# Turned tokens one tile a place, conversions shared from the fifth chunk on, and an overflow list in ten steps

## The chip, the cores and the metric

The kernel runs on one core of a Trainium2 chip. The metric is device time in microseconds (us) of one execution, the median of several. The core's engines run side by side, each through its own queue in order: TensorE (PE, matrix products, with weight loads PEld), VectorE (DVE), ScalarE (ACT), GpSimd (POOL) and SyncE (SP, which issues DMA transfers). An instruction that waits holds everything behind it on its engine.

## The reference

Clustered attention feeds a layer of 16 experts (4 groups of 4). A query attends only to keys of its own cluster; then every token goes to one expert, a two-layer network with ReLU, weighted by two softmax values:

```
mask = q_assign[:, :, :, None] == k_assign[:, :, None, :]
attn = softmax(where(mask, scale * q @ k.T, -1e9)) ; x = attn @ v     # 3072 tokens of 512
g_idx = argmax(x @ w_group) ; e_idx = argmax(xg @ w_expert[g])
h = np.maximum(xg[mask_e] @ w1[g, e], 0.0)                            # 512 -> 1024
out[tok_idx] = (g_w * e_w)[:, None] * (h @ w2[g, e])                  # 1024 -> 512
```

## The kernel before

Attention runs first, up to about 400 us. The expert stage is what the change touches. Float32 values are carried as two float16 parts, a high and a low one, so each product is three matmuls (high by high, high by low, low by high).

The first expert's 288 tokens of the first three batches are computed by `part_a`. Then `ranks` (L1421) goes over the remaining work in "ranks": rank -1 is a tile of 128 tokens of that first expert, ranks 0 to 14 are the other experts by falling size (288, 272, 256, 240, 232, 224, 216, 208, 200, 192 ... tokens). The body of a rank has eight places, i = 0 to 7. At each place PE computes one eighth of the rank's hidden layer (`up`, L1193, into one of three PSUM banks psh, evicted by ACT as hh, L1195, and by DVE as hl, L1196) and one eighth of the rank before's second layer (`down`, L1215 into one of two banks psy, evicted as yh on ACT and yl on DVE, L1219; some ranks take the form of L1229). At place 2 (place 6 of rank -1) `settle` turns the finished output back (L1251, into one of three banks psm), ACT scales it (y, L1257), and POOL scatters it to memory.

Weights come through `stream` (L994). Every expert has 16 chunks of 512 KB, loaded by SP (L951) into 13 lent places some way ahead; a chunk's place is free again when the chunk is split. Splitting (`split_chunk`, L972) takes two instructions: a conversion to the high part, on ACT (L978) or on POOL (L980), and the low part on DVE (L981). Chunks are counted from 0 here. `HI` alternates the two engines, but only from chunk `LEAD` = 12 on; chunks 0 to 11 are converted on ACT alone. Chunks 0 to 3, 4, 5, 8 and 9 are first-layer weights (wh0a, then wh0b), chunks 6, 7, 10 and 11 second-layer weights (wh1b). One chunk is split at each place.

A rank's tokens are gathered by POOL (L1150) from memory, token by token, and have to be turned for the products: PE transposes a tile of up to 128 tokens into a psm bank (L1165, or L1163 for a short one), and ACT copies it to xT (L1166; on DVE for the second tile in rank -1). `tokens` (L1168) does all tiles of the next rank at place `TOK` = 5, two or three of them.

For tokens that found no slot, DVE makes a list of further work (`lists` and `make_list`), in steps that ranks 2 and up take one at a time at place 3. Its long instructions work on 697 values of a single partition. The list is in eight steps: make_list's are taken in ranks 4 to 7, a test of the attention's sums in ranks 8 and 9.

The order in which instructions stand in an engine's queue is not the order of the code: a scheduler places them by its own estimate of times, under the `issue_after` constraints.

Of the kernel before, what the change touches and what calls it, by code (L numbers as in the profile page):

```python
# [11 lines left out]
F16 = mybir.dt.float16  # L12
# [10 lines left out]
P = 128  # L23
# [864 lines left out]
class Experts:  # L888
# [6 lines left out]
    short = ()  # L895
    AHEAD, MORE, AT = 9, 4, 8
    SLT = 13
    FILL, SETTLE, TOK = (0, 1, 2, 3, 4, 5, 6, 7), 2, 5
    HI = (0, 1, 0, 1, 0, 1, 0, 1)
    LEAD = 12  # L900

    def __init__(self, ctx, tc, R, w1, w2, out, stage, wa):
        self.tc, self.R, self.w1, self.w2, self.out = tc, R, w1, w2, out
# [212 lines left out]
    def stream(self):  # L1116
# [5 lines left out]
        for n in range(len(parts)):  # L1122
# [7 lines left out]
            if st is None:  # L1130
                yield
                continue
            self.split_chunk(st, *self.weights_of(r, i), i, q, self.HI[n % 8] if n >= self.LEAD else 0)
            self.ready = 4 * r + q + 1 if i == 0 else self.ready
# [32 lines left out]

    def tokens(self, xgs, M, beside=False):  # L1168
        nc = self.nc
        xT = self.xp.tile([P, 2, self.R.KD, M], F16, name="xT")  # L1170
        for t, xg in enumerate(xgs):
            self.transposed(xT, xg, t, min(P, M - t * P), self.R.psm.tile([P, 512], F32, name="psm"), nc.vector.tensor_copy if beside and t % 2 == 1 or M == P else nc.scalar.copy)
        return xT

    def ffn(self, xT, M, W, gcols, idcols):
        h = []
# [193 lines left out]
    def make_list(self):  # L1370
        nc, R = self.nc, self.R
        EB, MJ, MO = R.E + 1, R.N // P + 1, self.MO
        V = nc.vector
        V.tensor_tensor(out=self.Lrem, in0=self.c17[0:1], in1=self.done, op=ALU.subtract)
        V.tensor_tensor(out=self.Lgj, in0=self.Lrem.broadcast_to([1, EB, MJ]), in1=self.jt, op=ALU.is_gt)
        V.tensor_reduce(out=self.Lnov, in_=self.Lgj, axis=AX.X, op=ALU.add)
        V.tensor_tensor_scan(out=self.LhiE, data0=self.Lnov, data1=self.Lzer, initial=0.0, op0=ALU.add, op1=ALU.add)
        V.tensor_tensor(out=self.LloE, in0=self.LhiE, in1=self.Lnov, op=ALU.subtract)
        yield
        b3 = lambda x: x.unsqueeze(1).broadcast_to([1, MO, EB])  # L1380
        V.tensor_tensor(out=self.Lind, in0=self.jj, in1=b3(self.LloE), op=ALU.is_ge)
        V.tensor_tensor(out=self.Ltmp, in0=self.jj, in1=b3(self.LhiE), op=ALU.is_lt)
        V.tensor_tensor(out=self.Lind, in0=self.Lind, in1=self.Ltmp, op=ALU.mult)
        yield
        V.tensor_tensor(out=self.Ltmp, in0=self.Lind, in1=b3(self.eid), op=ALU.mult)
        V.tensor_reduce(out=self.Llst[:, 0], in_=self.Ltmp, axis=AX.X, op=ALU.add)
        yield

        V.tensor_tensor(out=self.Lsb, in0=self.base, in1=self.done, op=ALU.add)
        V.scalar_tensor_tensor(out=self.Lsb, in0=self.LloE, scalar=-float(P), in1=self.Lsb, op0=ALU.mult, op1=ALU.add)  # L1390
        V.scalar_tensor_tensor(out=self.Ltmp, in0=self.jj, scalar=float(P), in1=b3(self.Lsb), op0=ALU.mult, op1=ALU.add)
        V.scalar_tensor_tensor(out=self.Ltmp, in0=self.Ltmp, scalar=1.0 / 8, in1=self.Lind, op0=ALU.mult, op1=ALU.mult)
        V.tensor_reduce(out=self.Llst[:, 1], in_=self.Ltmp, axis=AX.X, op=ALU.add)
        V.tensor_copy(out=self.Llsi, in_=self.Llst)
        V.tensor_copy(out=self.Lnoi, in_=self.LhiE[:, EB - 1:EB])
        yield
# [24 lines left out]
    def ranks(self, bg):  # L1421

        E, sizes = self.R.E, self.sizes
        xT, xgs, down = self.xTB, self.xg0, iter(())
        for k in range(-1, E - 1):
            M = self.caps[k] if k >= 0 else P
            if 0 <= k < E - 2:
                xgs = self.gathers(k + 1)
            h = []
            up = self.up(xT, M, self.weights_of(k, 0) if k >= 0 else self.WA[0:2], h)  # L1430
            for i in range(8):
                while k >= 0 and self.ready < 4 * k + (4 if i >= 4 else 2) or k > 0 and self.ready2 < 4 * k - 4 + (4 if i >= 4 or not self.feature_major(self.caps[k - 1]) else 2):
                    next(self.fill)
                next(up, None)
                next(down, None)
                if i == (self.SETTLE if k >= 0 else 6):
                    if k == E - 2:
                        self.tc.keep_in_program_order(self.nc.gpsimd.drain())
                    self.settle()
                if i in self.FILL:  # L1440
                    with ExitStack() as order:
                        for op in (self.got, self.yev[min(1 + i // 2, 3)]) if k < 0 else (self.ev,):
                            order.enter_context(self.tc.issue_after(op.ins))
                        next(self.fill, None)
                if i == self.TOK and k + 1 < E - 1:
                    with self.tc.issue_after(self.mm.ins):
                        nT = self.tokens(xgs, self.caps[k + 1], k < 0)
                if k > 1 and i == 3:
                    with self.tc.issue_after(self.ev.ins):
                        next(bg, None)  # L1450
            for s in (up, down):
                for _ in s:
                    pass
            xT = nT
            if k >= 0:
                cols = [(self.gates[0:m, t, k:k + 1], self.ids[0:m, t, k:k + 1]) for t, m in enumerate(sizes[k])]
                down = self.down(h, M, self.weights_of(k, 1), [g for g, _ in cols], [i for _, i in cols])
            else:
                down = self.down(h, M, self.W2, [self.gB], [self.idB])
        for _ in self.fill:  # L1460
            pass
        for i, _ in enumerate(down):
            if i == 0:
                self.settle()
        self.settle()
        for _ in bg:
            pass

    def rest(self):
        self.again = True  # L1470
        nc, R, E, xp = self.nc, self.R, self.R.E, self.xp
        n_ov = nc.values_load(self.Lnoi[0:1, 0:1], min_val=0, max_val=self.MO)
        tabv = R.table.rearrange("(r s) w -> r s w", s=8)
        with self.tc.For_i(0, n_ov, 1) as j:
            er = self.load_reg(self.Llsi[0:1, 0, bass.ds(j, 1)], E - 1)
            tr = self.load_reg(self.Llsi[0:1, 1, bass.ds(j, 1)], (E + 1) * R.BS // 8 - P // 8)
            W = self.weights(er)
            tg = xp.tile([P, 2], F32, name="tg", bufs=1)
            nc.sync.dma_start(out=tg, in_=tabv[bass.ds(tr, P // 8)].rearrange("r s w -> (r s) w"))
            tid = xp.tile([P, 1], I32, name="tid", bufs=1)  # L1480
            nc.vector.tensor_copy(out=tid, in_=tg[:, 0:1])
            gt = xp.tile([P, 1], F32, name="gt", bufs=1)
            nc.vector.tensor_scalar(out=gt, in0=tg[:, 1:2], scalar1=1.0 / (XS * WS * WS), scalar2=None, op0=ALU.mult)
            xT = self.tokens([self.gather(tid, P)], P)
            for _ in self.ffn(xT, P, W, [gt], [tid]):
                pass

# [82 lines left out]
def tile_cluster_attention_moe(ctx, tc, qT, kT, vr, cen, wr, w1, w2, out):  # L1570
# [3 lines left out]
    E = w1.shape[0]  # L1574
# [17 lines left out]
    X = Experts(ctx, tc, R, w1, w2, out, stage, wa)  # L1592
# [15 lines left out]
    for i, _ in enumerate(ga):  # L1608
        with tc.issue_after(X.mm.ins):
            if i == X.SLT:  # L1610
                X.xTB = X.tokens([X.xB], P)

    def late():
        yield from X.lists()
# [35 lines left out]
```

## Time and profile before

| what | us |
|---|---|
| median of 3 runs | 746.83 (746.58 to 747.35) |
| the profiled execution | 744.5 |
| its span, first to last instruction | 742.7 |
| PE busy in the span | 715.7 (96%) |
| DVE busy | 602.7 (81%) |
| ACT busy | 480.8 (65%) |
| POOL busy | 499.4 (67%) |

The profile is of one execution, 2.3 us below the median of the timed ones, and 1.8 us of its time lie outside the span. PE's granted clock is full all through. Busy shares are means over the whole span; a timeline gives single instructions with start, duration and, in brackets, the idle time of the engine before them and what ended it.

### The profile page before, as it was taken

To read this page: it belongs to the slowest core of one execution; us is meant where nothing else is said; L and a number is where in the kernel's file an instruction comes from. 1 tells how busy PE (TensorE), PEld (TensorE's weight loads), DVE (VectorE), ACT (ScalarE), POOL (GpSimd) and SP (SyncE) were. 2 spreads that over 40 slices of the span, in tenths; PEclk is the share of its full clock that TensorE was granted. 3 is DMA by queue.
4 is the path that set the end of the run, shared out by engine and by line. 5 is a ranking of instruction groups with operands and counts; after the bars stand their busy time and mean duration, and the time that the engine had idled before them with its cause. 6 is when DMAs were issued, how large, how long until landed. Compare 5 with 4: busy or idle time off the path is not lost.

```text
span 742.7 us, 26654 instructions
## 1 busy us (share of the span) xinstructions
PE 715.7 (96%) x11068; PEld 617.5 (83%) x11068; DVE 602.7 (81%) x1221; ACT 480.8 (65%) x935; POOL 499.4 (67%) x493
## 2 busy tenths in 40 slices
PE   5999999999999999999999989999999999999996
PEld 3688888888888888888788776888789999999996
DVE  7898889799888997989876576766779989899951
ACT  4768877788778887677977285344445554555542
POOL 9999787777787877878786335454646685555632
PEclk9999999999999999999999999999999999999999
DMA  8655644435345351240510699967787787888401
GB/s 264 177 133 166 192 113 120 142 98 154 83 120 172 99 151 35 68 129 6 197 60 33 216 363 368 294 215 222 229 248 227 243 273 263 259 273 285 138 34 35
DMA packets 78616, 128.03 MB, mean 172 GB/s; under 512 B 7667, under 2 KB 45427, under 8 KB 78488
## 3 DMA queue, kind: packets, MB, share of 16 engines
q1 hardware_dynamic: 73404, 112.63, 49.6%
q0 software_dynamic: 4928, 13.59, 5.1%
q8 instruction: 88, 1.44, 0.8%
q14 instruction: 40, 0.33, 0.1%
q10 hardware_dynamic: 156, 0.03, 0.0%
HBM read 93.41 MB, written 13.65 MB: 144 GB/s over the span
## 4 chain that ended last, share of the span: by engine, by line
PE 56%; DVE 21%; issue 7%; ACT 6%; DMA 5%; POOL 3%; SPq 1%; POOLq 0%; DVEq 0%; ACTq 0%
PE psh L1193 11%; PE psy L1215 9%; DVE mpart L321 7%; PE pso L386 6%; PE pso L387 5%; PE psf L360 5%; PE psf L361 5%; PE psc L318 5%; DMA st<-w 3%; PE psy L1229 3%; DVE parts L213 2%; PE psm L700 1%; ACT p L365 1%; DMA wl<-w 1%; PE psm L1165 1%
## 5 line engine op out<-in xcount | busy, mean ns | idle before, releaser
L367 POOL TENSOR_TENSOR pl<-p 128x512 f16<-128x512 f32 x278 | 284.9, 1040 | 75.4 <-ACT p L365 70.9
L321 DVE TENSOR_REDUCE mpart<-psc 128x1 f32<-128x512 f32 (+1 forms) x282 | 190.5, 684 | 28.5 <-PE psc L318 28.1
L365 ACT ACTIVATE p<-psf 128x512 f32<-128x512 f32 x288 | 169.6, 596 | 50.2 <-PE psf L361 43.6
L386 PE MATMUL pso<-V,p 128*128 128x65 f16 x1152 | 160.2, 193 | 0.0
L387 PE MATMUL pso<-V,pl 128*128 128x64 f16 x1152 | 160.0, 194 | 0.0
L386 PE MATMUL pso<-V,pl 128*128 128x65 f16 x1152 | 159.5, 193 | 0.4 <-POOL pl L367 0.4
L387 PE MATMUL pso<-V,p 128*128 128x64 f16 x1152 | 159.2, 193 | 0.0
L360 PE MATMUL psf<-A 82*128 82x384 f16 (+2 forms) x576 | 142.6, 273 | 2.1 <-ACT p L365 1.8
L361 PE MATMUL psf<-B 128*128 128x384 f16 (+2 forms) x576 | 142.7, 273 | 0.0
L387 PEld LDWEIGHTS <-p 128*128 128x128 bf16 x1152 | 112.2, 97 | 22.0
L386 PEld LDWEIGHTS <-p 128*128 128x128 bf16 x1152 | 113.0, 98 | 9.4 <-issue 1.2
L386 PEld LDWEIGHTS <-pl 128*128 128x128 f16 x1152 | 112.5, 98 | 0.5 <-POOL pl L367 0.5
L387 PEld LDWEIGHTS <-pl 128*128 128x128 f16 x1152 | 111.5, 97 | 0.1
L318 PE MATMUL psc<-A 80*128 80x512 f16 (+1 forms) x376 | 108.1, 330 | 0.8 <-DVE mpart L321 0.4
L1195 ACT ACTIVATE hh<-psh 128x160 f16<-128x160 f32 (+14 forms) x136 | 46.5, 344 | 79.3 <-PE psh L1193 79.0
L1258 POOL DMA_INDIRECT out_dram<-y,ri x33 | 42.8, 1296 | 76.2 <-ACT y L1257 70.9
L1196 DVE SCALAR_TENSOR_TENSOR hl<-psh,hh 128x160 f16<-128x160 f32 (+14 forms) x136 | 49.8, 368 | 50.6 <-ACT hh L1195 50.3
L1193 PE MATMUL psh<-xT,wh0a 128*128 128x288 f16 (+7 forms) x512 | 74.6, 255 | 0.0
L1150 POOL DMA_INDIRECT xg<-xbuf,ri x25 | 42.8, 1710 | 43.9 <-PE psm L1165 30.6
L1193 PE MATMUL psh<-xT,wh0b 128*128 128x272 f16 (+6 forms) x448 | 64.7, 254 | 1.2 <-DVE hl L1196 1.2
L361 PEld LDWEIGHTS <-B 128*128 128x128 f16 x576 | 56.4, 98 | 11.2 <-issue 2.7
L1193 PE MATMUL psh<-xT,wl0a 128*128 128x288 f16 (+7 forms) x256 | 64.1, 255 | 0.0
(406 smaller groups left out, 1780.8 us busy)
## 6 DMA issues: line engine op xcount, KB each, us to landing
st<-w SPq DMA_DIRECT2D x67, 512.0 KB
xs<-w SPq DMA_DIRECT2D x29, 512.0 KB
B<-parts SPq DMA_DIRECT2D x64, 192.0 KB
wh<-w SPq DMA_DIRECT2D x16, 512.0 KB
wl<-w SPq DMA_DIRECT2D x16, 512.0 KB
kx<-kT SPq DMA_DIRECT2D x16, 384.0 KB
qx<-qT SPq DMA_DIRECT2D x16, 384.0 KB
vx<-vr SPq DMA_DIRECT2D x16, 384.0 KB
```

The source lines that it names most:

```text
L318: last["mm"] = nc.tensor.matmul(out=pc[:, off:off + k1 - k0], lhsT=QA[h % 8][0:80, c * P:(c + 1) * P], rhs=KA[h % 8][0:80, k0:k1], start=T ...
L321: nc.vector.tensor_reduce(out=(mp[:, 0, 0:1], mp[:, :, 1], mp[:, 1, 0:1])[i], in_=pc.rearrange("p (a x) -> p a x", a=n), axis=AX.X, op=ALU ...
L360: nc.tensor.matmul(out=o, lhsT=KA[h % 8][0:82, ks], rhs=QA[h % 8][0:82, q0:q1], start=True, stop=False)
L361: nc.tensor.matmul(out=o, lhsT=KBs[h][:, ks], rhs=QBs[h][:, q0:q1], start=False, stop=True)
L365: cfg["exp"] = nc.scalar.activation(out=p32, in_=pf, func=AF.Exp, scale=QK / (SQ * SQ))
L367: lo = (nc.vector if u in (EARLY if h < 2 else DVE_LO[h % 8] if h < NH - 2 else DVE_END) else nc.gpsimd).tensor_tensor(out=pl, in0=p32, in ...
L386: nc.tensor.matmul(out=O[:, col:col + 65], lhsT=p[:, bs], rhs=vh, start=c == 0 and q == 0 and i == 0, stop=False, skip_group_check=True)
L387: nc.tensor.matmul(out=O[:, col:col + 64], lhsT=p[:, bs], rhs=vl, start=False, stop=c == NCH - 1 and i == 1, skip_group_check=True)
L1193: self.mm = nc.tensor.matmul(out=ph[:, 0:M], lhsT=w[:, k, fs], rhs=xT[:, a, k], start=i == 0, stop=i == 3 * KD - 1)
L1195: nc.scalar.activation(out=hh[:, f], in_=ph[:, 0:M], func=AF.Relu)
L1196: self.ev = nc.vector.scalar_tensor_tensor(out=hl[:, f], in0=ph[:, 0:M], scalar=0.0, in1=hh[:, f], op0=ALU.max, op1=ALU.subtract)
L1215: self.mm = nc.tensor.matmul(out=py[:, 0:M], lhsT=w[:, f, d * P:(d + 1) * P], rhs=a[:, f], start=i == 0, stop=i == len(prods) - 1)
```

## The change

The tiles of the next rank's tokens are turned at one place each, the last of them at place 6: with three tiles at places 4, 5 and 6, with two at 5 and 6 (`TOK` = 7, and `tokens` yields after every tile). `LEAD` goes from 12 to 4, so that chunks 5, 7, 9 and 11 are converted on POOL and not on ACT. `make_list` yields twice more, so it takes six steps, in ranks 4 to 9, and the whole list ten.

```diff
-    FILL, SETTLE, TOK = (0, 1, 2, 3, 4, 5, 6, 7), 2, 5
+    FILL, SETTLE, TOK = (0, 1, 2, 3, 4, 5, 6, 7), 2, 7
...
-    LEAD = 12
+    LEAD = 4
...
     def tokens(self, xgs, M, beside=False):
         nc = self.nc
-        xT = self.xp.tile([P, 2, self.R.KD, M], F16, name="xT")
+        xT = self.xT = self.xp.tile([P, 2, self.R.KD, M], F16, name="xT")
         for t, xg in enumerate(xgs):
...
-        return xT
+            yield
...
         V.tensor_tensor(out=self.Lind, in0=self.jj, in1=b3(self.LloE), op=ALU.is_ge)
+        yield
         V.tensor_tensor(out=self.Ltmp, in0=self.jj, in1=b3(self.LhiE), op=ALU.is_lt)
         V.tensor_tensor(out=self.Lind, in0=self.Lind, in1=self.Ltmp, op=ALU.mult)
...
         V.scalar_tensor_tensor(out=self.Ltmp, in0=self.jj, scalar=float(P), in1=b3(self.Lsb), op0=ALU.mult, op1=ALU.add)
+        yield
         V.scalar_tensor_tensor(out=self.Ltmp, in0=self.Ltmp, scalar=1.0 / 8, in1=self.Lind, op0=ALU.mult, op1=ALU.mult)
...
-                if i == self.TOK and k + 1 < E - 1:
+                if i == self.TOK - len(xgs) and k + 1 < E - 1:
+                    turn = self.tokens(xgs, self.caps[k + 1], k < 0)
+                if i >= self.TOK - len(xgs) and k + 1 < E - 1:
                     with self.tc.issue_after(self.mm.ins):
-                        nT = self.tokens(xgs, self.caps[k + 1], k < 0)
+                        next(turn, None)
...
-            xT = nT
+            xT = self.xT
```

The remaining hunks adapt the other two callers of `tokens`, which turn one tile, to the generator.

What this does to the queues is seen at three places. The first is ACT in rank -1, where the hidden tiles are 128x128. The rows are the difference from before; wh0b and wh1b are the high parts of chunks, st and xs the places that they were loaded to, xT the turned tokens of rank 0.

```order
-L978 ACTIVATE wh1b<-st 128x4x256 x2
+L978 ACTIVATE wh1b<-st 128x4x256
 L1195 ACTIVATE hh<-psh 128x128 x2
 L978 ACTIVATE wh0b<-xs 128x2x512
 L1195 ACTIVATE hh<-psh 128x128
-L1166 COPY xT<-psm 128x8x128
-L1166 CAST xT<-psm 128x8x32
-L978 ACTIVATE wh0b<-st 128x2x512
+L978 ACTIVATE wh1b<-st 128x4x256
 L1195 ACTIVATE hh<-psh 128x128
+L1166 COPY xT<-psm 128x8x128
+L1195 ACTIVATE hh<-psh 128x128 x2
```

Before, the copy of the first turned tile stood behind the conversion of chunk 8 (wh0b<-xs); now chunk 10 (the added wh1b<-st) stands ahead of it too, and the last, short tile comes behind the three scalings of `settle`. The second place is DVE in the same rank, at the first hidden tiles.

```order
+L981 SCALAR_TENSOR_TENSOR wl0b<-xs,wh0b 128x2x512
 L1219 SCALAR_TENSOR_TENSOR yl<-psy,yh 128x288
+L1196 SCALAR_TENSOR_TENSOR hl<-psh,hh 128x128
 L981 SCALAR_TENSOR_TENSOR wl0b<-st,wh0b 128x2x512
-L1196 SCALAR_TENSOR_TENSOR hl<-psh,hh 128x128 x3
-L981 SCALAR_TENSOR_TENSOR wl0b<-xs,wh0b 128x2x512
-L981 SCALAR_TENSOR_TENSOR wl1b<-st,wh1b 128x4x256
 L1196 SCALAR_TENSOR_TENSOR hl<-psh,hh 128x128 x2
```

The split of chunk 5 (wl0b<-xs) moved ahead of the first eviction hl, and now waits for POOL's conversion. The third place is DVE in rank 9 (hidden tiles 128x192), where the long list instructions now stand; wl1a is a low part of second-layer weights. In the changed file the list's lines have numbers one or two higher than before.

```order
 L1196 SCALAR_TENSOR_TENSOR hl<-psh,hh 128x192
 L981 SCALAR_TENSOR_TENSOR wl1a<-wh_12091,wh1a 128x4x256
-L1511 COPY zf<-psm 128x1
+L1394 SCALAR_TENSOR_TENSOR Ltmp<-Ltmp,Lind 1x697
+L1397 CAST Lnoi<-LhiE 1x1
+L1196 SCALAR_TENSOR_TENSOR hl<-psh,hh 128x192
+L1395 TENSOR_REDUCE Llst<-Ltmp 1x41
 L1219 SCALAR_TENSOR_TENSOR yl<-psy,yh 128x200
```

The eviction yl, which stood behind a one-value copy, now stands behind two passes over 697 values. In rank 7 the same happens with the list's step of ranks 6 before (two passes ahead of yl), while three passes that stood behind yl there have gone to ranks 8 and 9.

## Rows read from the trace of the kernel before

**Rows 1.** The page's head and its first part, busy time of each engine.

```profile
span 742.7 us, 26654 instructions
PE 715.7 (96%) x11068; PEld 617.5 (83%) x11068; DVE 602.7 (81%) x1221; ACT 480.8 (65%) x935; POOL 499.4 (67%) x493
```

**Rows 2.** Waits of PE in the expert stage: sum, count, longest.

```profile
PE psh L1193 <- DVE hl L1196: 2.1, 3, 1.2
...
PE psy L1215 <- DVE yl L1219: 1.9, 1, 1.9
...
PE psm L1251 <- ACT xT L1166: 1.1, 1, 1.1
```

**Rows 3.** Timeline of PE: start, duration, instruction, [idle before <-what ended it].

```profile
438.60 0.27 PE L1193 MATMUL psh<-xT,wh 128*128 128x128 f16 x2 [0.45 <-DVE hl L1196]
...
440.52 0.22 PE L1251 MATMUL psm<-back,yh 128*128 128x128 f16 x1 [1.09 <-ACT xT L1166]
...
442.53 0.41 PE L1193 MATMUL psh<-xT,wh0a 128*128 128x288 f16 x2
...
461.51 0.41 PE L1193 MATMUL psh<-xT,wh0b 128*128 128x272 f16 x2 [1.21 <-DVE hl L1196]
...
607.05 0.91 PE L1215 MATMUL psy<-hh,wh1b 128*128 128x216 f16 x8
...
613.46 0.87 PE L1215 MATMUL psy<-hh,wh1a 128*128 128x208 f16 x8 [1.93 <-DVE yl L1219]
...
645.49 0.85 PE L1215 MATMUL psy<-hh,wh1b 128*128 128x200 f16 x8
```

**Rows 4.** Window of rank -1: PE, PEld, DVE, ACT, POOL busy, clock, DMA, GB/s.

```profile
430.00:442.50 12.50, 10.50 (x163) 9.52 (x161) 9.98 (x18) 10.28 (x19) 3.75 (x4) 1.00 1.07 369
```

**Rows 5.** Timeline of ACT, ranks -1 and 0.

```profile
437.00 1.06 ACT L978 ACTIVATE wh1b<-st 128x1024 f16<-128x1024 f32 x1 [1.13 <-DMA st<-w]
...
439.31 0.26 ACT L1195 ACTIVATE hh<-psh 128x128 f16<-128x128 f32 x1
...
439.47 1.00 ACT L1166 COPY xT<-psm 128x1024 f16<-128x1024 f16 x1
...
440.36 0.38 ACT L1166 CAST xT<-psm 128x256 f16<-128x256 f32 x1
...
441.74 1.80 ACT L1257 ACTIVATE y<-psm,Ag 128x512 f32<-128x512 f32 x3
...
450.25 1.06 ACT L978 ACTIVATE wh1a<-xs 128x1024 f16<-128x1024 f32 x1 [3.30 <-DMA xs<-w]
...
455.97 1.06 ACT L978 ACTIVATE wh1a<-wh 128x1024 f16<-128x1024 f32 x1 [3.12 <-DMA wh<-w]
```

**Rows 6.** Timeline of POOL, ranks 0 and 6.

```profile
458.95 1.05 POOL L980 TENSOR_SCALAR wh1a<-wh 128x1024 f16<-128x1024 f32 x1
...
586.93 9.13 POOL L1150 DMA_INDIRECT xg<-xbuf,ri  x1 [2.43 <-PE psm L1165]
```

**Rows 7.** Timeline of DVE, ranks -1 and 0.

```profile
433.42 1.23 DVE L981 SCALAR_TENSOR_TENSOR wl0b<-st,wh0b 128x1024 f16<-128x1024 f32 x1 [0.37 <-ACT wh0b L978]
...
445.92 0.46 DVE L1196 SCALAR_TENSOR_TENSOR hl<-psh,hh 128x288 f16<-128x288 f32 x1 [1.89 <-ACT hh L1195]
```

**Rows 8.** Timeline of DVE, ranks 6, 7 and 9.

```profile
585.50 0.87 DVE L1385 TENSOR_TENSOR Ltmp<-Lind,eid 1x697 f32<-1x697 f16 x1
...
598.43 2.06 DVE L981 SCALAR_TENSOR_TENSOR wl0a<-st,wh0a 128x1024 f16<-128x1024 f32 x1 [2.94 <-POOL wh0a L980]
...
602.45 3.75 DVE L981 SCALAR_TENSOR_TENSOR wl1a<-st,wh1a 128x1024 f16<-128x1024 f32 x1
...
606.35 0.36 DVE L1219 SCALAR_TENSOR_TENSOR yl<-psy,yh 128x216 f16<-128x216 f32 x1
...
640.39 3.55 DVE L981 SCALAR_TENSOR_TENSOR wl1a<-wh,wh1a 128x1024 f16<-128x1024 f32 x1
...
643.94 0.35 DVE L1219 SCALAR_TENSOR_TENSOR yl<-psy,yh 128x200 f16<-128x200 f32 x1
```

More of the change, by code (lines that the diff above doesn't have):

```diff
@@ L1483, in rest @@
             nc.vector.tensor_scalar(out=gt, in0=tg[:, 1:2], scalar1=1.0 / (XS * WS * WS), scalar2=None, op0=ALU.mult)
-            xT = self.tokens([self.gather(tid, P)], P)
+            next(self.tokens([self.gather(tid, P)], P))
+            xT = self.xT
             for _ in self.ffn(xT, P, W, [gt], [tid]):
@@ L1610, in tile_cluster_attention_moe @@
             if i == X.SLT:
-                X.xTB = X.tokens([X.xB], P)
+                next(X.tokens([X.xB], P))
+                X.xTB = X.xT
     def late():
```

## The prediction, made before the changed kernel ran

> **What bounds the kernel now.** I read the page's first part first: PE is busy 715.7 of 742.7 us, DVE 602.7, POOL 499.4, ACT 480.8 [rows 1]. So PE's queue sets the end, and an edit counts by the idle time that it opens or closes on PE. The waits of PE in the expert stage come second; the reader is to see how few there are: hidden tiles wait for hl three times (2.1 us together, one of 1.2) and the second layer once for yl (1.9) [rows 2]. Third, PE's timeline gives the places. The output of rank -1 is turned back at 440.52 after 1.09 us of waiting for a copy on ACT, rank 0 starts at 442.53, there is a wait of 1.21 at 461.51, and one of 1.93 at 613.46 in rank 7 [rows 3]. All that could be gained there is some 5 us. What could be lost has no such end, so I looked next at what runs close beside PE.
>
> In rank -1 that is ACT and the weights' transfers. From 430 to 442.5 ACT is busy 10.28 of 12.5 us and the DMA share is 1.07 at 369 GB/s [rows 4]: the transfers are the limit, and a chunk of 128x1024 float32 values (0.524 MB) arrives every 0.524/0.369 = 1.42 us. ACT already waits for them: the conversion at 437.00, of chunk 7, waited 1.13 for its DMA, later ones 3.30 and 3.12 [rows 5].
>
> **The change, part by part.** *Conversions to POOL, tiles turned singly.* Chunks 5, 7, 9 and 11 leave ACT: four conversions of 1.06 [rows 5] go, and as many of 1.05 appear on POOL [rows 6]. That does not bring ACT's work forward, since what it converts is bound to arrivals, and order matters more than amount. Before, the copy of rank 0's first turned tile stood behind chunk 8 and ran at 439.47 [rows 5]. Now it stands behind chunk 10. If chunk 7 was there at 437.00, chunk 10 is there at 437.00 + 3 x 1.42 = 441.3. From then on ACT is a chain, by the steps from start to start in [rows 5]: the conversion 1.0, an eviction hh 0.16, the copy 0.9, to 443.4. PE's turning back waits for that copy's bank, as it does at 440.52 [rows 3]. The first of the three scalings y follows some 0.7 later (a third of the 1.3 us of turning back, and two evictions hh), at 444.1; the scalings take 1.7 and the cast of the short tile, now behind them, 0.38 (it ran before them at 440.36) [rows 5]. Rank 0's products read every tile, so they start at about 446.15 and not at 442.53 [rows 3]: **+3.6 us**. Bounds: if chunk 10 is already there when ACT comes to it (about 439.6, after the hh at 439.31 [rows 5]), the same chain of 4.85 ends at 444.4, +1.9. If chunks come as slowly as up to the conversion at 450.25 (chunk 14, so 13.25/7 = 1.9 each [rows 5]), chunk 10 is there at 442.7, +5.0. I take 3.6, from the window of the stretch itself.
>
> Something comes back. The wait of 1.21 at 461.51 [rows 3] has its root in the conversion at 455.97, which waited 3.12 for a transfer [rows 5]. With saturated queues that transfer does not come later because PE does, so a PE that is 3.6 late finds it done: **-1.2**. No other wait stands between there and rank 7 in [rows 2], so the rest, 2.4, is carried on.
>
> DVE takes the split of chunk 5 ahead of the first hl, and waits there for POOL (1.05 [rows 6]) beside its own 1.23 [rows 7]; behind it the three hl and the next splits queue, and PE waits for hl. It may cost PE up to 1.3 at the first hidden tiles, but these us lie before the copy that is late anyway, and DVE idles 1.89 us soon after [rows 7]. I cost it at nothing; without that cover (were chunk 10 early) it is those 1.3.
>
> The trace shows four-fold what a POOL conversion can do to a split: splits of 1.23 [rows 7] became 3.75 and 3.55 at 602.45 and 640.39 [rows 8]. The Trainium skill (SBUF — State Buffer, sections "SBUF: two separate sides" and "Who interferes with whom") says that VectorE and GpSimd share a pair of ports as an exclusive lock, held for a whole instruction, whenever a VectorE instruction has two inputs in SBUF and GpSimd reads SBUF too. The long splits agree with it, and by that rule the four added conversions would block DVE by up to 4 x 1.05 = 4.2 us; the sum would be up to that much higher if none of it met idle time. The sum here does without it, since DVE has idle time at that place.
>
> *The list in ten steps.* A pass over 697 values of one partition takes 0.87 [rows 8], about 0.8 from start to start. The steps now stand elsewhere, and two places are close. Rank 9: the split at 640.39 lasts until 643.94, where yl begins [rows 8]. Now two passes, a copy of one value and an hl come between: 0.8 + 0.05 + 0.27 + 0.8 = 1.9, so yl ends at 643.94 + 1.9 + 0.35 = 646.2. PE needs it at 645.49 [rows 3], or a little sooner as a turned tile has moved behind that place. That opens a wait of 0.7 to 1.0; I take **+0.8**, between 0 (if the split is short this time) and 1.9.
>
> Rank 7: before, POOL's gather at 586.93 took 9.13 us [rows 6], so POOL's conversions came late, DVE idled 2.94 until 598.43, ran the long split of 602.45 and delivered yl at 606.35 [rows 8], 0.34 before PE's 607.05 [rows 3]. Three passes behind it made the wait of 1.93 [rows 3]. Now these three are gone, but two passes and an hl stand ahead of yl: 606.35 + 0.8 + 0.8 + 0.27 + 0.36 = 608.6, a wait of 1.55 in place of 1.93: **-0.3**, between -1.9 (the long gather does not recur, nothing is late) and +0.3 (the later hidden tiles wait as well). Ranks 5 and 6 exchange a step for one of like length; ranks 8, 10 and 11 get short pieces: nothing, at most one pass, 0.87.
>
> The sum: 3.6 - 1.2 - 0.3 + 0.8 = **+2.9 us**. The profiled execution of 744.5 us (a span of 742.7 and 1.8 around it) would become 747.4. The median of the runs is 746.83, 2.3 more, so the forecast is 749.7.
>
> **The rivals.** *First: the long gather does not come back.* Its 9.13 us are no property of the code, and the steps around it have moved. Then rank 7's wait goes wholly: 3.6 - 1.2 - 1.9 + 0.8 = +1.3, 748.1. For it: one execution shows it once. Against it: the gather stood ready behind the same PE release, and its surroundings on DVE are still full of passes.
>
> *Second, the other side: faster.* The early weights arrive sooner than the chain has it, because POOL's conversions free lent places and SP can issue earlier. It decides if chunk 10 is there before ACT has finished chunk 8 and could copy by 439.5 plus what four conversions save. Then PE's waits of 0.45 and 1.09 near 440 shrink, rank 0 starts up to 0.6 earlier, and with rank 7's 1.93 gone and rank 9 within its slack the sum is up to -2.5; about -1.9, 744.9. Against it: the DMA share of 1.07 [rows 4]. Places don't hold these transfers up, the transfers themselves do.
>
> *Third: slower still.* Chunk 10 comes at 442.7, and DVE's late hl adds to it: +5.0 - 1.2 - 0.3 + 0.8 = +4.3, 751.1, with one more pass in the way 752. For it: the slow arrivals up to 450.25 [rows 5]. Against it: most of that slowness is behind chunk 10, by the 1.42 of the window.
>
> *Fourth: nothing to see.* The late start of rank 0 is taken up by waits further on that are due to transfers, as 1.21 of it is, and rank 9 stays within its slack: 3.6 - 1.2 - 1.9 - 0.5 = 0, 746.8. Against it: [rows 2] hold no further waits to give.
>
> **How the numbers follow.** Two versions can be told apart from about 0.2%, 1.5 us. The forecast gets 0.54, with a range of its own from 748.2 to 751.2; the first rival 0.18, the second 0.12, the third 0.10, the fourth 0.06. The range from 746.0 to 751.8 leaves out the second rival and the far part of the third, less than 2 in 10. Faster is the second rival, 0.12, and a trace of the fourth: 0.13. No change (745.3 to 748.3) holds the rest of the fourth, somewhat over half of the first and a tail of the forecast: 0.20. Slower: 0.67.
>
> **What would show it.** Right: in the profile of the changed kernel ACT's conversion ahead of the first copy of rank 0's tokens waits for a DMA until about 441.3, the copy runs at 442.5 and not at 439.47, rank 0's first product starts near 446, and the wait at 461.51 is gone from PE. A yl of rank 9 shows a wait of PE of about 0.8, and one of rank 7 about 1.5. Wrong: rank 0 starts before 444 (the chain on ACT fails), a transfer that is as late for rank 1 as before (the 1.2 does not come back), or splits of DVE in rank -1 of 2 us and more that PE waits for (POOL collides where I gave it nothing).

## The result: 7.8 us slower, and the profile after

The changed kernel takes 754.47 us (median of 4, 753.32 to 756.0) against 746.71 of the kernel before (4, 746.49 to 747.35): a ratio of 1.0104, 95% interval 1.0083 to 1.0124. Run again later beside other kernels it gave 1.0091 (1.0066 to 1.0115). The direction was forecast, the size was not: 749.7 with a range to 751.8. One correction to the text ahead of the prediction: an expert has 8 chunks of 512 KB, not 16; the forecast used the chunks' arrivals, not that number.

The head of the page after. Against [rows 1] DVE is 5 us busier with the same operations, and POOL 8, of which four more conversions make up some 4; the time of an instruction that is held counts as busy.

```profile
span 754.2 us, 26657 instructions
PE 722.3 (96%) x11068; PEld 621.5 (82%) x11068; DVE 607.3 (81%) x1221; ACT 480.4 (64%) x931; POOL 507.5 (67%) x497
```

The waits of PE in the expert stage (sum, count, longest), to be held against [rows 2]: where yl was late once, it is late seven times.

```profile
PE psy L1215 <- DVE yl L1219: 5.5, 7, 2.3
PE psh L1193 <- DVE hl L1196: 1.4, 2, 1.0
PE psh L1193 <- issue: 0.9, 1, 0.9
PE psy L1215 <- DVE hl L1196: 0.8, 2, 0.4
PE psm L1251 <- ACT xT L1166: 0.7, 1, 0.7
```

Where they stand, in PE's timeline; 442.53, 461.51, 607.05, 613.46 and 645.49 of [rows 3] are the 449.34, (no wait), 612.56, (no wait) and 651.71 of this one.

```profile
430.34 1.14 PE L1215 MATMUL psy<-hh,wh1a 128*128 128x288 f16 x8 [1.91 <-DVE yl L1219]
...
445.68 0.22 PE L1251 MATMUL psm<-back,yh 128*128 128x128 f16 x1 [0.71 <-ACT xT L1166]
...
449.34 0.41 PE L1193 MATMUL psh<-xT,wh0a 128*128 128x288 f16 x2 [0.87 <-issue]
...
612.56 0.90 PE L1215 MATMUL psy<-hh,wh1b 128*128 128x216 f16 x8 [0.18 <-DVE yl L1219]
651.71 1.05 PE L1215 MATMUL psy<-hh,wh1b 128*128 128x200 f16 x8 [2.31 <-DVE yl L1219]
...
694.72 0.24 PE L1215 MATMUL psy<-hl,wh1a 128*128 128x176 f16 x1 [0.44 <-DVE hl L1196]
696.11 0.77 PE L1215 MATMUL psy<-hh,wh1a 128*128 128x176 f16 x8 [0.28 <-DVE yl L1219]
704.97 0.77 PE L1215 MATMUL psy<-hh,wh1a 128*128 128x176 f16 x8 [0.25 <-DVE yl L1219]
```

Waits alone don't add up to the loss, since PE also loses by its clock. So I took the start of the same product (L1193, counted from the first one) in two traces and subtracted: the lag is how much later the product starts than in the kernel before. The lag of the changed kernel is 2.77 us at the start of the stage (405.09 in before), 5.22 at 461.51, 3.67 at 614.53, 3.98 at 632.82, 8.07 at 651.03 and 11.08 at 703.79 and to the end. The steps between are the change's terms:

| stretch, by the times of before | forecast | after | after, second run |
|---|---|---|---|
| ahead of the stage, to 405 | 0 | +2.8 | +1.0 |
| ranks -1 and 0, 405 to 461 | +2.4 | +2.4 | +2.7 |
| rank 7's wait, 461 to 614 | -0.3 | -1.5 | -1.6 |
| 614 to 633 | 0 | +0.3 | +0.3 |
| rank 9, 633 to 651 | +0.8 | +4.1 | +4.1 |
| ranks 10 to 13, 651 to 704 | 0 | +3.0 | +3.0 |

The first line is not the change's. PE's granted clock was 0.50 between 25 and 30 us (2.4 GHz is 1.00), in attention, which is the same code, and the lag was 1.0 to 2.6 at 405 in every one of the 15 further profiles, of whatever version, with and without such a spell. The profiled execution of before, 2.3 us below its own median, was the quick one.

The columns of this row are the length of the stretch, busy us (and count) of PE, PEld, DVE, ACT and POOL, then clock, DMA share and GB/s.

```profile
25.00:30.00 5.00, 4.89 (x29) 3.01 (x27) 4.26 (x9) 2.47 (x5) 4.55 (x5) 0.50 0.92 212
```

**Ranks -1 and 0** went in the order that the chain on ACT said: the conversion ahead of the copy waits for its DMA, the copy starts at 444.62, which without the 2.77 is 441.85 (forecast 442.5), and the short tile's cast, forecast behind the scalings, is at 448.92. Rank 0's first product at 449.34 is 446.6 on the old clock, against 446.15 forecast and 442.53 in [rows 3].

```profile
429.39 0.71 ACT L1218 ACTIVATE yh<-psy 128x288 f16<-128x288 f32 x2 [6.18 <-PE psy L1215]
...
443.50 1.06 ACT L978 ACTIVATE wh1b<-st 128x1024 f16<-128x1024 f32 x1 [1.94 <-DMA st<-w]
...
444.62 1.00 ACT L1166 COPY xT<-psm 128x1024 f16<-128x1024 f16 x1
...
448.92 0.37 ACT L1166 CAST xT<-psm 128x256 f16<-128x256 f32 x1 [0.82 <-PE psh L1193]
```

The first of these rows is a second thing that isn't the change's. ACT took its first eviction yh at 429.39, long after PE's product (PE waited for it from 428.4 on), and PE lost 1.91. The same came in four of the 15 later profiles, all four of one batch on one chip, one of them of the kernel before without its list passes (e11_nopass), where nothing is changed up to there. I found no cause for it in the trace. It stands in the +2.4 and, since rank 0 waits for weights anyway, only partly adds to it.

The one profile of a three-part kernel without it, f3_all_act, is the better test of the chain, since it is the same code up to rank 6. Its conversion of chunk 10 (first row) and rank 0's first product (second) stand at 440.1 and 445.0 on the old clock (its own lag at 405 is 1.65), where 441.3 and 446.15 were forecast: rank 0 is 2.5 late and not 3.6, and +0.9 are left at 461.

```profile
441.77 1.06 ACT L978 ACTIVATE wh1b<-st 128x1024 f16<-128x1024 f32 x1 [1.67 <-DMA st<-w]
...
446.68 0.41 PE L1193 MATMUL psh<-xT,wh0a 128*128 128x288 f16 x2
```

One profile's step up to 461 is good to some 0.7 us only: without a late yh, kernels that convert the early chunks as before have it between -0.4 and +0.9 in the table below.

**Rank 9** is DVE's, to be read against [rows 8]. As forecast, pass, hl and pass stand between the held split and yl. But yl starts 7.4 us later than in before, and PE came only 4.0 later. DVE was behind already when it came to the split: that starts 5.3 later (645.73 against 640.39). The first row shows where from: in rank 8 DVE stood idle 1.69 for a conversion on POOL.

```profile
641.75 2.06 DVE L981 SCALAR_TENSOR_TENSOR wl0a<-st,wh0a 128x1024 f16<-128x1024 f32 x1 [1.69 <-POOL wh0a L980]
...
645.73 3.75 DVE L981 SCALAR_TENSOR_TENSOR wl1a<-wh,wh1a 128x1024 f16<-128x1024 f32 x1
649.40 0.87 DVE L1394 SCALAR_TENSOR_TENSOR Ltmp<-Ltmp,Lind 1x697 f32<-1x697 f32 x1
...
650.53 0.85 DVE L1395 TENSOR_REDUCE Llst<-Ltmp 1x41 f32<-1x697 f32 x1
651.31 0.34 DVE L1219 SCALAR_TENSOR_TENSOR yl<-psy,yh 128x200 f16<-128x200 f32 x1
```

That conversion stood behind a long gather of the next rank's short tile, the third one in three ranks:

```profile
633.16 7.47 POOL L1150 DMA_INDIRECT xs<-xbuf,ri  x1 [1.30 <-PE psm L1163]
640.65 1.07 POOL L980 TENSOR_SCALAR wh0a<-st 128x1024 f16<-128x1024 f32 x1
```

Behind the wait PE's granted clock fell to 0.50 (1.2 GHz of 2.4), which cost another 1.3 to 1.7 us (0.40 + 0.50 + 0.50 + 0.31 in the four us from 652 by the granted clock; 1.3 is the rise of the lag behind the wait in e5_turnlist). Columns as above.

```profile
652.00:653.00 1.00, 1.00 (x10) 0.94 (x8) 1.00 (x2) 0.00 (x0) 0.00 (x0) 0.60 0.50 182
653.00:654.00 1.00, 1.00 (x14) 0.95 (x13) 1.00 (x2) 0.16 (x1) 0.00 (x0) 0.50 0.00 0
654.00:655.00 1.00, 1.00 (x8) 0.95 (x7) 1.00 (x4) 0.73 (x2) 0.92 (x1) 0.50 0.73 203
655.00:656.00 1.00, 1.00 (x10) 0.97 (x9) 0.97 (x1) 0.94 (x2) 0.47 (x2) 0.69 0.91 332
```

**Ranks 10 to 13** were in no term. PE's turning of a short tile (first fence) and POOL's queue (second) show why DVE (third) is late there: the next gather of a short tile starts at 672.18, 0.66 behind the start of the turning, the two conversions stand behind it, and a split that began just before them is held 3.60. The gather's row names DVE as what ended its wait; that it hangs on the turning is seen from the 0.66, which is the same in e2_turn (663.26 and 663.92) and e7_tok6 (661.83 and 662.49). From rank 11 on there are two such held splits a rank (3.76 and 3.56 in rank 11), where before had one.

```profile
671.52 0.36 PE L1163 MATMUL psm<-ident,xs 128*128 128x48 f16 x8
```

```profile
672.18 1.74 POOL L1150 DMA_INDIRECT xs<-xbuf,ri  x1 [3.74 <-DVE hl L1196]
673.94 1.07 POOL L980 TENSOR_SCALAR wh0a<-wh 128x1024 f16<-128x1024 f32 x1
674.96 1.06 POOL L980 TENSOR_SCALAR wh1a<-wl 128x1024 f16<-128x1024 f32 x1
```

```profile
673.50 3.60 DVE L981 SCALAR_TENSOR_TENSOR wl1a<-st,wh1a 128x1024 f16<-128x1024 f32 x1
...
683.39 3.76 DVE L981 SCALAR_TENSOR_TENSOR wl1a<-wl,wh1a 128x1024 f16<-128x1024 f32 x1
```

### The profile page after: what moved, and what is told of

It is laid out like the page before. It is cut to its first block, busy times and chain, and to the rows that moved or that the text cites. A ratio compares the mean times of both kernels' runs of the same rounds, so it can differ in the third digit from the quotient of the medians.

```text
span 754.2 us, 26657 instructions
## 1 busy us (share of the span) xinstructions
PE 722.3 (96%) x11068; PEld 621.5 (82%) x11068; DVE 607.3 (81%) x1221; ACT 480.4 (64%) x931; POOL 507.5 (67%) x497
## 4 chain that ended last, share of the span: by engine, by line
PE 56%; DVE 23%; issue 8%; ACT 5%; POOL 4%; DMA 3%; POOLq 0%; DVEq 0%; ACTq 0%; SPq 0%
PE psh L1193 12%; PE psy L1215 8%; DVE mpart L321 6%; PE pso L386 6%; PE pso L387 5%; PE psf L360 5%; PE psf L361 5%; PE psc L318 5%; PE psy L1229 3%; DVE wl1b L981 2%; DVE parts L213 2%; PE psm L700 1%; DVE wl1a L981 1%; DMA st<-w 1%; POOL parts L199 1%
## 5 line engine op out<-in xcount | busy, mean ns | idle before, releaser
L360 PE MATMUL psf<-A 82*128 82x384 f16 (+2 forms) x576 | 144.4, 276 | 2.0 <-ACT p L365 1.9
L361 PE MATMUL psf<-B 128*128 128x384 f16 (+2 forms) x576 | 144.5, 276 | 0.0
L1258 POOL DMA_INDIRECT out_dram<-y,ri x33 | 40.4, 1224 | 68.9 <-ACT y L1257 63.4
L1193 PE MATMUL psh<-xT,wh0a 128*128 128x288 f16 (+7 forms) x512 | 74.7, 255 | 0.9 <-issue 0.9
L1150 POOL DMA_INDIRECT xg<-xbuf,ri x25 | 46.3, 1854 | 37.2 <-PE psm L1165 20.6
L1193 PE MATMUL psh<-xT,wh0b 128*128 128x272 f16 (+6 forms) x448 | 65.5, 256 | 0.0
L360 PEld LDWEIGHTS <-A 82*128 82x128 f16 x576 | 56.3, 99 | 10.5 <-issue 2.3
```

The costliest lines, as they stand in the source:

```text
L360: nc.tensor.matmul(out=o, lhsT=KA[h % 8][0:82, ks], rhs=QA[h % 8][0:82, q0:q1], start=True, stop=False)
L361: nc.tensor.matmul(out=o, lhsT=KBs[h][:, ks], rhs=QBs[h][:, q0:q1], start=False, stop=True)
L1193: self.mm = nc.tensor.matmul(out=ph[:, 0:M], lhsT=w[:, k, fs], rhs=xT[:, a, k], start=i == 0, stop=i == 3 * KD - 1)
```

## The experiments

Times are ratios to the kernel before, run on the same chip beside it. The other columns are the steps of the lag, taken as above from one profile each. "Late yh" marks profiles with ACT's late first eviction; it is worth 2.1 us at 432, and 3.8 in e12_ten and e13_all6, where the granted clock fell to 0.50 for some 3 us behind it.

| kernel | ratio (95%) | 405-461 | 461-614 | 614-633 | 633-651 | 651-704 |
|---|---|---|---|---|---|---|
| e1_lead | 1.0030 (1.0018-1.0042) | +2.1 | 0 | 0 | 0 | 0 |
| e2_turn | 1.0011 (0.9998-1.0023) | -0.3 | -1.9 | 0 | 0 | +2.4 |
| e3_list | 1.0008 (0.9997-1.0019) | -0.4 | -0.7 | 0 | +1.5 | 0 |
| e5_turnlist | 1.0063 (1.0045-1.0080) | -0.3 | -1.5 | +0.3 | +4.1 | +3.0 |
| e7_tok6 | 0.9984 (0.9972-0.9997) | 0 | -1.5 | 0 | 0 | 0 |
| e8_tok6list | 1.0000 (0.9988-1.0011) | -0.4 | -2.0 | 0 | +1.5 | 0 |
| e9_act | 0.9969 (0.9950-0.9987) | +0.9 | -1.8 | 0 | 0 | 0 |
| e10_list9 | 1.0067 (1.0047-1.0086) | -0.4 | -1.5 | +3.0 | 0 | +1.8 |
| e11_nopass | 0.9974 (0.9957-0.9991) | +0.6, late yh | -2.1 | 0 | 0 | 0 |
| e12_ten | 1.0014 (1.0000-1.0028) | +5.4, late yh | 0 | 0 | 0 | 0 |
| e13_all6 | 1.0006 (0.9989-1.0023) | +4.5, late yh | -2.0 | 0 | +1.5 | 0 |
| after_again | 1.0091 (1.0066-1.0115) | +2.7, late yh | -1.6 | +0.3 | +4.1 | +3.0 |
| f1_turnlist_act | 0.9970 (0.9957-0.9984) | -0.4 | -2.1 | 0 | 0 | 0 |
| f2_tok6_act | 0.9974 (0.9961-0.9988) | -0.2 | -2.1 | 0 | 0 | 0 |
| f3_all_act | 0.9998 (0.9986-1.0011) | +0.9 | -2.1 | 0 | 0 | 0 |

**The parts alone.** The kernel before with one part of the change, and the change without the conversions.

```diff
e1_lead       -    LEAD = 12            +    LEAD = 4
e2_turn       only the hunks of TOK = 7, tokens and its callers
e3_list       only the two yields in make_list
e5_turnlist   the change with LEAD = 12
```

> The kernel before with LEAD = 4 alone: chunks 5, 7, 9 and 11 are converted on POOL, tiles are turned and the list is made as before. Theory of parts (each part has its own price, as read from the changed kernel's trace): chunk 10's conversion stands ahead of the copy of rank 0's first tile here too, so rank 0 starts 3.5 to 4 us later against the start of the expert stage, the wait of 1.2 near 461 is gone, and +2.4 us are left: 749.1. Rank 7 keeps its wait of 1.9 and ranks 9 to 14 show no waits of PE. Rival (the conversions on POOL disturb all that follows): waits of PE for yl and hl of 0.2 to 2.3 appear in ranks 9 to 14 as in the changed kernel, and the time is 752 or more.

It held in size: +2.1 in the stage, 1.0030 timed, rank 7's wait unchanged at 1.93. PE waits 1.80 for hl at 437.19 and 2.02 for the copy at 443.80 (before: 0.46 and 1.09). The first of these is the split of chunk 5 ahead of hl, whose up to 1.3 the prediction had set at nothing. Behind the second the granted clock fell to 0.50 for some 3 us: from there to rank 0's first product PE took 3.58 us (443.80 to 447.38) and not 2.01 (440.52 to 442.53). So 1.6 of the 3.5 us by which rank 0 is late are the clock's, which is in no term: that the sum came out is in part luck.

> The kernel before with the turned tiles at one place each alone (TOK = 7 and the yield in tokens; LEAD stays 12, the list stays in eight steps). Theory of parts: on ACT the copy of rank 0's first tile stands behind chunk 8 as before, only the short tile's cast (0.38) comes behind the three scalings, so rank 0 starts 0 to 0.5 us later and the rest is unchanged: 746.7 to 747.2. Rival (turning at later places makes PE meet yl and hl earlier and takes the slack of ranks 9 to 14): PE waits of 0.2 to 0.4 per rank near the end, 748.5 to 750.

The median, 746.73, is the theory's; the trace is the rival's. Rank 7's wait of 1.93 goes, and 2.4 us come at the end, with the waits of 0.21 to 0.37 that the changed kernel has. Neither was in the price of this part, which was 0 to 0.5.

> The kernel before with the two further yields in make_list alone. Theory of parts: rank 7's wait shrinks by about 1.5 us, rank 9 waits about 2.3 for yl behind two passes and has a spell of half clock after it (1.5), and ranks 10 to 14 wait 0.25 to 0.45 twice a rank (3.3 together): +5 to +6, 752. Rival (the loss of ranks 9 to 14 needs the other parts, which bring DVE late to rank 9): a wait of at most 1 in rank 9, none behind it, and with rank 7's gain 745.5 to 747.5.

The rival held in time, 746.62, and nothing comes behind rank 9; the wait there is 1.35, more than its 1. Rank 7 still waits, 1.26 in place of 1.93, near the 1.55 of the prediction: alone, the list does there what the working said.

> The changed kernel with LEAD = 12: only the conversions of chunks 5, 7, 9 and 11 go back to ACT. Theory of parts: all but the 2.4 us of rank 0: 752 if the loss of ranks 9 to 14 is the list's. Rival (the losses are not additive; the later start of rank 0 or the turned tiles decide in which phase the ranks meet): below 749, with waits at other ranks than in the changed kernel. By both the granted clock of the first 40 us may fall to half for some us as in the changed kernel's profiled execution, or not, since nothing there has changed; where it does, up to 2.8 us are lost ahead of the expert stage.

The theory held: 751.26, with all of the loss behind rank 7. The parts don't add up: e2_turn and e3_list lose 0.8 and 0.6 us by their ratios, together they lose 4.7, which is more than the intervals can explain. What turning does to POOL's queue is the likely reason, and the next runs test it.

**One place earlier.** e7_tok6 and e8_tok6list are e2_turn and e5_turnlist with one number changed, so that the last tile is turned at place 5, as in before.

```diff
-    FILL, SETTLE, TOK = (0, 1, 2, 3, 4, 5, 6, 7), 2, 7
+    FILL, SETTLE, TOK = (0, 1, 2, 3, 4, 5, 6, 7), 2, 6
```

> One tile a place alone, as in e2_turn, but one place earlier (TOK = 6: two tiles at places 4 and 5, three at 3, 4 and 5); LEAD 12, list in eight steps. Theory (POOL's queue: the gather of the second tile waits for its turning, the two conversions stand behind it, and turning at place 6 brings them 1.1 us later, into a split of DVE that they then hold for 3.6 us): with the last tile at place 5 the conversions start as in the kernel before, ranks 11 to 14 show one held split a rank instead of two and no wait of PE, the 2.4 us that e2_turn lost there stay, and with rank 7's gain the stage is 1 to 2.5 us shorter than before's: 744 to 745.5. Rival (turning singly itself, by its smaller pieces on PE and ACT, makes the tail): waits of 0.2 to 0.4 a rank in ranks 11 to 14 as in e2_turn, 746 to 747.

The theory held, 744.78: no wait of PE behind rank 7. POOL and DVE have parted again as in before (681.52 and 683.53 there). One rank on from the place that was shown above, where the changed kernel holds one split for 3.56, the two conversions start in two different splits, which take 1.83 and 1.80, together 1.2 us more than undisturbed ones and not 2.4. The POOL rows:

```profile
679.11 1.74 POOL L1150 DMA_INDIRECT xs<-xbuf,ri  x1 [0.16 <-issue]
681.56 1.04 POOL L980 TENSOR_SCALAR wh0b<-xs 128x1024 f16<-128x1024 f32 x1 [0.71 <-PE psh L1193]
682.58 2.00 POOL L980 TENSOR_SCALAR wh1b<-st 128x1024 f16<-128x1024 f32 x1
```

and DVE beside them:

```profile
681.84 1.83 DVE L981 SCALAR_TENSOR_TENSOR wl1b<-xs,wh1b 128x1024 f16<-128x1024 f32 x1
...
683.85 1.80 DVE L981 SCALAR_TENSOR_TENSOR wl1b<-st,wh1b 128x1024 f16<-128x1024 f32 x1
```

> As e7_tok6 with the list in ten steps. Theory (DVE is behind PE by a fixed amount after the long gathers; a wait that PE doesn't have in rank 7 it has in rank 9, where two passes stand ahead of yl): a wait of 2.0 to 2.3 in rank 9, the granted clock at half for some 3 us behind it, and no waits in ranks 11 to 14: e7_tok6 plus 2 to 4.4, 747 to 749. Rival (rank 9's wait came from turning at place 6): below 1 us of wait in rank 9, the time within 0.7 of e7_tok6.

Neither: 745.95, a wait of 1.36 in rank 9 (as in e3_list) and no fall of the clock. So about 1 us of the wait of 2.31, the clock's 1.3 and the tail belong to turning at place 6; 1.4 is the list's, where 0.8 was forecast. DVE (first row) is the difference: by the lag of PE it comes to the split 0.6 later than in before here (640.05, at a lag of -0.95), and 1.4 later in the changed kernel (645.73, at 3.98). The third long gather ends 0.7 earlier against PE here (634.96 and 640.63), and its turning stands 2.1 earlier (625.41 and 632.45).

```profile
640.05 3.74 DVE L981 SCALAR_TENSOR_TENSOR wl1a<-wh,wh1a 128x1024 f16<-128x1024 f32 x1
...
646.03 0.85 PE L1215 MATMUL psy<-hh,wh1b 128*128 128x200 f16 x8 [1.36 <-DVE yl L1219]
```

**POOL or the passes.** In e9_act, f1_turnlist_act, f2_tok6_act and f3_all_act late chunks are converted on ACT, in e11_nopass the list's long passes are gone: it leaves the entries of the overflow list out, and would be of no use where a token finds no slot.

```diff
 e9_act: e2_turn, f1: e5_turnlist, f2: e7_tok6, f3: the changed kernel
-  self.HI[n % 8] if n >= self.LEAD else 0)
+  self.HI[n % 8] if self.LEAD <= n < 92 else 0)      # e9_act; 60 in f1, f2 and f3
 e11_nopass: the kernel before
-  the eight operations on 697 values and three short ones, L1381 to L1394
+  V.memset(self.Llsi, 0)
```

> e2_turn, but chunks from 92 on (ranks 10 and later) are all converted on ACT, none on POOL. Theory (splits held by POOL's conversions make the tail): no split of DVE over 2 us from rank 10 on, no wait of PE for yl or hl there that DVE causes, 2.4 us less than e2_turn, 744.5; if ACT with its four more conversions of 1.06 a rank gets late itself, waits named after ACT appear instead. Rival (the tail is the evictions' order on DVE, not the held splits): waits of 0.25 to 0.37 stay although splits take 1.2.

The theory held, 744.38: no split is held from rank 10 on, and the tail of 2.4 us is gone.

> e5_turnlist (LEAD 12, turning and list as in the change), but chunks from 60 on (rank 6 and later) are all converted on ACT. Theory (the list's loss in ranks 7 to 9 and the tail come from POOL: its conversions stand behind gathers of 7 to 9 us, come late, and hold DVE's splits for 3.6 us; the passes alone cost little): the gathers may stay long, but no split waits for POOL, rank 9's wait falls from 2.3 to under 0.5 (in this order one pass and not two stands ahead of its yl, worth 0.8 of that), no fall of the clock, no tail: 7 us less than e5_turnlist's stage, 744 to 745. Rival (the passes themselves make DVE late): a wait of 1.4 or more stays in rank 8 or 9, 747 or more. A second rival: ACT with four conversions of 1.06 more a rank gets late, and PE waits for hh or xT.

The theory held, 743.69 against 751.26 of e5_turnlist: the passes are all there, and cost nothing. Its DVE in rank 9 reaches yl at 641.40, some 3 us before PE needs it (645.49 in before, less the lag of 0.8):

```profile
639.41 1.21 DVE L981 SCALAR_TENSOR_TENSOR wl1a<-wh,wh1a 128x1024 f16<-128x1024 f32 x1
640.55 0.87 DVE L1394 SCALAR_TENSOR_TENSOR Ltmp<-Ltmp,Lind 1x697 f32<-1x697 f32 x1
...
641.40 0.34 DVE L1219 SCALAR_TENSOR_TENSOR yl<-psy,yh 128x200 f16<-128x200 f32 x1
```

And the gathers aren't long any more, although DVE runs the same operations: 1.71 where e5_turnlist has 7.43 (587.92) and before had 9.13 [rows 6].

```profile
588.19 1.71 POOL L1150 DMA_INDIRECT xg<-xbuf,ri  x1 [4.52 <-PE psm L1165]
```

> The changed kernel, all three parts, with chunks from 60 on converted on ACT. Theory: what is left of its loss is chunk 10's conversion ahead of rank 0's first copy, 2.1 to 2.4 us, less rank 7's wait of 1.9 which goes: 746.5 to 747.5, at most 1 us above the kernel before. Rival (the early conversions on POOL shift DVE in later ranks too): 749 or more.

A little better than the theory, 745.61, a ratio of 0.9998: the whole loss of the change but its early conversions goes with POOL's later ones. Those early ones can be timed here: f3_all_act is 1.9 us above f1_turnlist_act, which differs from it in LEAD alone.

> e7_tok6 (one tile a place up to place 5, list in eight steps, LEAD 12) with chunks from 60 on converted on ACT. Theory: rank 7's remaining wait of 0.4 goes, nothing else was left to gain there: 0 to 0.7 us less than e7_tok6, so 744 to 745 and 1 to 2.5 less than the kernel before. Rival (ACT gets late): 0.5 or more above e7_tok6.

744.08, within the theory.

> The kernel before without the list's eight long passes (the entries of the overflow list are left out and set to zero, its count is kept; with no overflow the output is the same). Theory (the passes and the splits keep DVE busy without a gap, and POOL's gather of 9 us in rank 6 ends only where DVE first idles; from it come the late conversions and rank 7's wait): the gather takes under 5 us, rank 7's wait of 1.9 goes, the stage is about 2 us shorter: 744. Rival (the gather is long for the transfers' sake, whatever DVE does): a gather of 9 us and a wait of over 1 us in rank 7 stay.

The theory held: no gather over 4 us, no wait in rank 7, 745.26. In these runs a gather is long only where DVE has the list's passes and POOL the rank's conversions; that the two are enough isn't shown.

**The rest.** e10_list9 is e5_turnlist without the second of the new yields; e12_ten is e1_lead with `1 if n == 10 else` ahead of `self.HI[n % 8]`; e13_all6 is the changed kernel with TOK = 6; after_again is the changed kernel.

> e5_turnlist (LEAD 12, turning as in the change) with the first of the two new yields alone: the list in nine steps, its last passes in rank 8 and not in rank 9. Theory (rank 9 waits because two passes stand ahead of its yl, behind a held split): no wait of 2.3 in rank 9 and no half clock after it, 4.4 us go there; three passes now stand in rank 8, behind its yl, and may bring a wait of up to 1.5; the tail of 3.0 stays: 747 to 749 against 751.3. Rival (DVE is late by then in any case): a wait of about 2 in rank 8 or 9 and the clock's fall as before, 750 or more.

The rival held: the wait moved to rank 8, 2.41, without a fall of the clock behind it, and the time stays at 750.11. That DVE is behind anyway, wherever the passes stand, fits this; no run shows it by itself.

> e1_lead with chunk 10 on POOL as well, so that no conversion that waits for chunk 10 stands ahead of the copy of rank 0's first tile on ACT. Theory (that order alone is the 2.1 us of e1_lead): the copy runs at about 440.5 plus the run's early offset, rank 0 starts within 0.5 us of before's place in the stage, the stage is as long as before's: 746.2. Rival (POOL's conversions of chunks 5 and 7 hold DVE's splits and with them the hidden tiles' evictions hl): rank 0 starts 1 to 2 us late all the same, 747.5 or more.

Open. Its profile has the late yh and waits for hl of 0.57 to 1.45 in ranks -1 and 0, as the rival has it; timed it is at 1.0014, between the kernel before and e1_lead, and the intervals don't part it from either.

> The changed kernel with one number different: TOK = 6, so the last turned tile of every rank is at place 5 and not at 6. Theory (the change's loss is 2.1 of chunk 10's conversion, 4.4 of rank 9 and 3.0 of the held splits at the end, less 1.5 of rank 7, and turning at place 6 makes the tail and about half of rank 9): 2.1 more than e8_tok6list, 748, with one wait of 1.4 in rank 9 and none behind it. Rival (the later start of rank 0 shifts the phase of POOL against DVE in all ranks): waits in ranks 11 to 14 and 750 or more.

The waits are the theory's: one of 1.38 in rank 9, no tail. The price isn't: the 748.13 meets the forecast because the kernel before was slower beside it, and by the ratios the early conversions cost 0.4 us over e8_tok6list, give or take 1.5, and not 2.1. With TOK = 6 the first tile is turned earlier, and its copy (441.75) stands ahead of chunk 10's conversion (442.82) again. The profile's +4.5 is mostly the late yh and the clock behind it, 3.8; PE also waits 1.0 to 1.2 for hl three times up to rank 1.

> The changed kernel once more, unaltered. Theory (the half clock at 23 to 33 us and the late first eviction yh at 429.4 are accidents of that one execution, the rest is the change's): the first product of the stage's place at 405 comes anywhere between 405 and 408, no wait of 1.9 at 430, rank 9's wait of 2.3 with the clock's fall and the tail of 3 come again; 752 to 755. Rival (the early loss belongs to the changed program): 2.8 us are lost ahead of the expert stage again, and the wait at 430 is there.

The change's steps repeat within 0.1 us from 461 on. The lag at 405 was 1.0 and not 2.8, the clock fell again in rank 9; the late yh, which I had called an accident of one execution, came again, and in this batch in all four profiles.

## Why the prediction was wrong in size

**Right, with some luck:** that PE's few waits leave little to gain, the order on ACT (chunk 10 ahead of the copy), and that the wait at 461.51 comes back as gain. The sum of this term, forecast +2.4, was measured at +2.1 alone and +2.4 to +2.7 in the changed kernel; but the first holds 1.6 us of half clock and the others the late yh, neither of which the working has. Without both, f3_all_act shows +0.9 in its profile; timed, the part costs 2.0 (e1_lead) and 1.9 (f3_all_act over f1_turnlist_act). One sign of being wrong was seen too: the split at 436.03 was held for 2.06, and PE waited 1.00 for the hl behind it. It cost less than that, since rank 0 waits for chunk 10 in any case.

**Too small a gain:** rank 7, -0.3 forecast, -1.5 found. I took the long gather and its consequences as given and put the two passes ahead of yl behind them. In fact turning alone takes that wait away (e2_turn, -1.9): the first gather ended after 7.4 us and not 9.1, 1.7 sooner on before's clock, and the conversions behind it came sooner against PE. Why it ended then isn't shown.

**The step that failed, first:** rank 9 at +0.8. The working placed and sized the two passes rightly (1.8 us from the split's end to yl, 1.9 forecast), but measured them against PE's slack of before, as if DVE came to that split no later against PE. It came 1.4 later, and the split was 0.2 longer; with the 0.8 that makes the wait of 2.31. DVE is behind because in ranks 6, 7 and 8 the gathers held POOL's queue for 7.4, 9.2 and 7.5 us, where before had only 4.8 and 9.1, in ranks 5 and 6, and DVE waited for the conversions behind them. Without such conversions the wait is gone (f1_turnlist_act); with tiles turned one place earlier it is 1.36. That PE no longer waits in rank 7 doesn't explain it: e8_tok6list gains 2.0 there, more than the 1.5 here, and waits less in rank 9. Of the 4.1 us, 2.31 are the wait, 1.3 or more the clock behind it, which no term had.

**The step that failed, second:** the turned tiles at nothing. I followed them on PE and ACT, and not their third consequence: POOL's gather of the next tile waits for the turning, and POOL's conversions stand behind that gather. A turning one place later moves two conversions by more than a us, into a single split. e7_tok6 (one place earlier) and e9_act (no conversions there) each take the 2.4 to 3.0 us away. The rule on the port that I weighed (the Trainium skill, SBUF — State Buffer, "Who interferes with whom") agrees with these held splits, 3.60 where an undisturbed one takes 1.2, but I looked for it at the wrong place: I priced it in rank -1 at up to 4.2 us and set it at 0 there, and didn't ask where else the change moves a conversion.

**The rivals:** none had this. "Slower still" had a later chunk 10, not a DVE that is behind in rank 9. The chances gave slower 0.67; the range ended 2.7 us too low.

## What to carry to other kernels

When a step moves on one engine, follow what waits for it through every queue that it feeds, and ask what stands behind the waiting instruction: here a transposition released a gather, and the gather two conversions. Where two engines hold each other up, count the overlaps and not only the work: the same conversions cost a DVE split 0.6 us each when they met two splits, and 2.4 when both met one. And slack measured in the trace of before holds only as long as the engine that it is measured against isn't later itself; the version that took POOL out of the way (f1_turnlist_act, 0.9970) beat both kernels, with all the list's passes still on DVE.

## What the runs showed of the hardware

A gather that POOL issues can last until DVE runs out of work. The one at 611.58 in the changed kernel took 9.18 us and ended at 620.76; DVE's first gap in that time began at 620.18, when it ran out of work, because the conversion that it needed stood behind the gather (POOL first, then DVE).

```profile
611.58 9.18 POOL L1150 DMA_INDIRECT xg<-xbuf,ri  x1 [2.30 <-PE psm L1165]
621.06 0.96 POOL L1150 DMA_INDIRECT xg<-xbuf,ri  x1 [0.30 <-DMA wh<-w]
622.03 1.08 POOL L980 TENSOR_SCALAR wh0b<-wl 128x1024 f16<-128x1024 f32 x1
```

```profile
619.81 0.37 DVE L1196 SCALAR_TENSOR_TENSOR hl<-psh,hh 128x200 f16<-128x200 f32 x1
623.14 2.06 DVE L981 SCALAR_TENSOR_TENSOR wl0b<-wl,wh0b 128x1024 f16<-128x1024 f32 x1 [2.96 <-POOL wh0b L980]
```

The Trainium skill (SBUF — State Buffer, "SBUF: two separate sides") has a like trap, transfers issued by GpSimd that starve while VectorE holds the shared ports, told for another kind of VectorE instruction. These rows agree with the effect: 9.2 us beside such a DVE, 1.7 in f1_turnlist_act.

It is no rule, though. Of the 33 gathers over 4 us in the stage, in all 17 profiles, 27 ended 0.5 to 0.9 us behind DVE's first gap; the other six, of 7.43 to 7.46, ended without one, the gather at 592.14 in the changed kernel among them. And other gathers are short although DVE has no gap: 1.74 at 672.18 in the changed kernel, 1.27 at 589.13 in e11_nopass. What decides it stays open here.

PE's granted clock fell to half after the waits of 2.29 and 2.31 in rank 9 (e5_turnlist and the changed kernel) and after those of 1.98, 2.00 and 2.02 around rank -1 (e13_all6, e12_ten, e1_lead), but not after six of 1.90 to 1.93, and not after one of 2.41 in rank 8 (e10_list9). What decides it stays open here.
